# First steps of attention loaded in fp32 on the hardware queues, DMA issues pinned to program order, and w_out held back

## The chip, the cores and the metric

The kernel runs on one core of one Trainium2 chip. The metric is the time of one execution on the device in microseconds (us); a median is over all timed runs of a kernel. Every job also ran the kernel before on the same chip. The profile is one execution; its span runs from the first instruction to the last and is about 1.7 us shorter than the time of the same execution. The profile's names for the engines are PE (matmuls), DVE (VectorE), ACT (ScalarE), POOL (GpSimd) and SP (SyncE, which here only issues DMAs). In its lines `ps_s` are the scores, `ps_o` the attention sums, `ps_h` the projection into 2048; `qT` and `xblk` are q and x after their transposes, `v_f` is v in fp32.

A run counts as slow when it is over 1.5% above the fastest of the same kernel. With one core there is no other die to compare with, so this goes by the times alone.

## The reference, cut to what matters

```python
# q, k, v: (4, 8, 768, 64); window 128, 4 sink positions
scores = q @ k.T / sqrt(64)
keep   = (pos < 4) | ((0 <= rel) & (rel < 128))
x      = softmax(where(keep, scores, -1e9)) @ v      # -> (3072, 512)
h      = x @ w_in                                    # 512 -> 2048
P      = a0 + a1*h + a2*h**2 + a3*h**3
Q      = 1 + |b0|*|h| + |b1|*h**2
out    = (P / (Q + 1e-6)) @ w_out                    # 2048 -> 512
```

The output is 3072 x 512 in fp32. The kernel computes in bf16.

## The kernel before

It works in 12 steps of 256 tokens, each cut into two "units". One loop iteration holds the scores of one step, the attention sums of an earlier one and the projections of earlier ones, so that all engines have work. A tile scheduler orders the instructions of each engine, and that order need not be the program's.

```python
def load_q(tile_i):                    # 24 tiles of 128 tokens; 3 buffers
    t_ = a_kv.tile([P, H, D], BF16, tag="q_bf", name="q_bf", bufs=3)
    nc.gpsimd.dma_start(out=t_, in_=q[b, :, T*P:(T+1)*P, :]...)   # fp32 -> bf16 in flight
# load_k: two DMAs per step, 2 buffers; load_v: eight DMAs per step, 3 buffers

def turn_q(tile_i):                    # a tile's buffer comes free when this has run
    nc.sync.dma_start_transpose(out=qT_fix[b % 2][:, :, T*P:(T+1)*P], in_=q_bf.pop(tile_i)...)

def turn_x(s, grp):                    # x of a step in two groups, two DMAs each
    for n in range(NTS):
        nc.sync.dma_start_transpose(out=xblk[s][:, 2*grp:2*grp+2, n*P:(n+1)*P],
                                    in_=x_n[s][:, n, grp*2*P:(grp+1)*2*P])

for i in range(-3, NU + 4):            # (cut; s_q, s_a: steps of scores and of attention)
    if grp_q == 0: feed(s_q + 2)       # loads of k and two q tiles
    scores(s_q, 2 * grp_q)
    project_in(i, 0); attend(s_a, 2 * grp_a)
    scores(s_q, 2 * grp_q + 1)
    project_in(i, 1); attend(s_a, 2 * grp_a + 1)
    turn_x(s_a, grp_a)
    if grp_q == 0: load_v(s_q + 1)
    mask(s_q, grp_q)
    ...
    if grp_q == 1:                     # the last thing before the next step's scores
        turn_q(2 * s_q + 3); turn_q(2 * s_q + 4)
        turn_k(s_q + 1)
    ...
```

The softmax here doesn't subtract the row's maximum and nothing guards it: scores larger than these inputs give would overflow.

Of the kernel before, what the change touches and what calls it, by code (L numbers as in the profile page):

```python
# [9 lines left out]
FP32 = mybir.dt.float32  # L10
BF16 = mybir.dt.bfloat16
U32 = mybir.dt.uint32
AF = mybir.ActivationFunctionType
# [4 lines left out]
def kernel(  # L18
# [13 lines left out]
    nc = tc.nc  # L32
    nc.scalar.preload_act_table_set("natural_log_exp_and_others")

    B, H, S, D = q.shape
    NS = int(n_sink)
    P = 128
    DM = moe_w_in.shape[0]
    DF = moe_w_in.shape[1]
    NDMC = DM // P  # L40
    NFFC = DF // P
    NPB = H // 2
    TS = 256
    GPB = S // TS
    NSTEP = B * GPB
    NTS = TS // P
    NHF = TS // 64
    EW = 256
    UC = NFFC // 2
    UW = UC * TS  # L50
    NU = 2 * NSTEP
    inv_sqrt_d = 1.0 / float(D) ** 0.5

    const_pool = ctx.enter_context(tc.tile_pool(name="const", bufs=1))
    wpool = ctx.enter_context(tc.tile_pool(name="weights", bufs=1))
    a_kv = ctx.enter_context(tc.tile_pool(name="a_kv", bufs=2))
# [8 lines left out]
    ps_mp = ctx.enter_context(tc.tile_pool(name="ps_m", bufs=2, space=bass.MemoryType.PSUM))  # L65


    k_bf, v_bd, q_bf, qT_b = {}, {}, {}, {}
    v_fix = []
    for n in range(3):  # L70
        t_ = const_pool.tile([P, NPB, NHF, 2, D + 1], BF16, name=f"v_bd_{n}")
        nc.gpsimd.memset(t_, 0.0)
        for e in range(2):
            nc.gpsimd.memset(t_[e * 64:(e + 1) * 64, :, :, e, D:D + 1], 1.0)
        v_fix.append(t_)

    def load_q(tile_i):
        b, T = divmod(tile_i, S // P)
        t_ = a_kv.tile([P, H, D], BF16, tag="q_bf", name="q_bf", bufs=3)
        nc.gpsimd.dma_start(out=t_, in_=q[b, :, T * P:(T + 1) * P, :].rearrange("h p d -> p h d"))  # L80
        q_bf[tile_i] = t_

    def load_k(s):
        b, g = divmod(s, GPB)
        t_ = a_kv.tile([P, NTS, H * D], BF16, tag="k_bf", name="k_bf")
        for t in range(NTS):
            r0 = g * TS + t * P
            nc.gpsimd.dma_start(out=t_[:, t, :].rearrange("p (h d) -> p h d", h=H),  # L88
                                in_=k[b, :, r0:r0 + P, :].rearrange("h p d -> p h d"))
        k_bf[s] = t_  # L90

    def load_v(s):
        b, g = divmod(s, GPB)
        t_ = v_fix[s % 3]
        for h in range(H):
            i, e = divmod(h, 2)
            nc.gpsimd.dma_start(  # L97
                out=t_[e * 64:(e + 1) * 64, i, :, e, 0:D],
                in_=v[b, h, g * TS:(g + 1) * TS, :].rearrange("(j p) d -> p j d", p=64))
        v_bd[s] = t_  # L100


    b_bc = const_pool.tile([P, 2], FP32, name="b_bc")
    nc.sync.dma_start(out=b_bc, in_=moe_b.partition_broadcast(P))
    a_bc = const_pool.tile([P, 4], FP32, name="a_bc")
    nc.sync.dma_start(out=a_bc, in_=moe_a.partition_broadcast(P))

    for n in range(3):
        load_q(n)
    load_k(0)  # L110
    load_v(0)

    ident = const_pool.tile([P, P], BF16, name="ident")
    make_identity(nc, ident)

    edge = const_pool.tile([P, 2, 64], BF16, name="edge")
    nc.gpsimd.memset(edge, 1.0)
    for e in range(2):
        lo = e * 64
        nc.gpsimd.affine_select(  # L120
            out=edge[lo:lo + 64, 0, :], in_=edge[lo:lo + 64, 0, :], pattern=[[1, 64]],
            compare_op=ALU.is_ge, fill=0.0, base=0, channel_multiplier=-1)
        nc.gpsimd.affine_select(
            out=edge[lo:lo + 64, 1, :], in_=edge[lo:lo + 64, 1, :], pattern=[[-1, 64]],
# [49 lines left out]
    for grp in range(2):  # L174
        for n in range(2):
            t_ = const_pool.tile([P, 2 * NHF * EW + 64], BF16, name=f"e_{grp}_{n}")
# [3 lines left out]
    for n in range(2):  # L180
        t_ = const_pool.tile([P, NPB * NHF, P], BF16, name=f"kT_{n}")
# [3 lines left out]
    for n in range(2):  # L185
        t_ = const_pool.tile([P, NPB, P], BF16, name=f"k_sink_{n}")
        nc.vector.memset(t_, 0.0)
        k_sink.append(t_)
    qT_fix = []
    for n in range(2):  # L190
        t_ = const_pool.tile([P, NPB, S + P], BF16, name=f"qT_{n}")
# [8 lines left out]
    def load_w_in(half):  # L200
        f0, f1 = half * DF // 2, (half + 1) * DF // 2
        for c in range(NDMC):
            t_f = a_kv.tile([P, DF // 2], FP32, tag="w_in_f", name="w_in_f", bufs=2)
            nc.sync.dma_start(out=t_f, in_=moe_w_in[c * P:(c + 1) * P, f0:f1])
            nc.vector.tensor_scalar(out=w_in_sb[c][:, f0:f1], in0=t_f, scalar1=csc,
                                    scalar2=None, op0=ALU.mult)

    def load_w_out():
        for c in range(NFFC):
            nc.gpsimd.dma_start(out=w_out_sb[c], in_=moe_w_out[c * P:(c + 1) * P, :])  # L210

    def load_v_sink():
        for h in range(H):
            nc.gpsimd.dma_start(out=v_sink[16 * h:16 * h + NS, :, h, 0:D],
                                in_=v[:, h, 0:NS, :].rearrange("b s d -> s b d"))
        for b in range(B):
            nc.vector.tensor_copy(out=v_sink[:, b, :, D], in_=ind)


    def turn_q(tile_i):  # L220
        b, T = divmod(tile_i, S // P)
        nc.sync.dma_start_transpose(out=qT_fix[b % 2][:, :, T * P:(T + 1) * P],
                                    in_=q_bf.pop(tile_i).rearrange("p h d -> p (h d)"))

    def turn_k(s):
# [60 lines left out]
    x_n = {}  # L286
# [31 lines left out]
    xblk = {}  # L318

    def turn_x(s, grp):  # L320
        if grp == 0:
            xblk[s] = xpool.tile([P, NDMC, TS], BF16, tag="xblk", name="xblk")
        for n in range(NTS):
            nc.sync.dma_start_transpose(  # L324
                out=xblk[s][:, 2 * grp:2 * grp + 2, n * P:(n + 1) * P],
                in_=x_n[s][:, n, grp * 2 * P:(grp + 1) * 2 * P])

# [64 lines left out]
    def project_out(m, tt, part):  # L392
        if part == 0:
            ps_out[m, tt] = ps_mp.tile([P, DM], FP32, tag="ps_m", name="ps_out")
        for fc in range(part * UC, (part + 1) * UC):
            u, fl = divmod(fc, UC)
            co = fl * TS + tt * P
            nc.tensor.matmul(ps_out[m, tt], lhsT=g_of[m, u][:, co:co + P], rhs=w_out_sb[fc],  # L398
                             start=(fc == 0), stop=(fc == NFFC - 1))
        if part == 1:  # L400
            o_t = o_sb.tile([P, DM], FP32, tag="o_t", name="o_t")
            nc.scalar.activation(out=o_t, in_=ps_out[m, tt], func=AF.Copy)
            row0 = m * TS + tt * P
            nc.sync.dma_start(out=out[row0:row0 + P, :], in_=o_t)



# [3 lines left out]
    def feed(s):  # L411

        load_k(s)
        for n in (2 * s + 1, 2 * s + 2):
            if n < NQT:
                load_q(n)
# [2 lines left out]
    feed(1)  # L419
    load_v_sink()  # L420
    load_w_in(1)
    load_w_out()
    for n in range(3):
        turn_q(n)
    turn_k(0)
    for i in range(-3, NU + 4):
# [4 lines left out]
        has_m = 0 <= i < NU  # L431
        back = i - 3
        has_o = 0 <= back < NU
        if has_q and grp_q == 0 and s_q + 2 < NSTEP:
            feed(s_q + 2)
        if has_q:
            scores(s_q, 2 * grp_q)
# [25 lines left out]
        if has_m:  # L463
            magnitude(i)
            square(i)
            denominator(i)
        if has_o:
            project_out(back // 2, back % 2, 0)
        if has_q and grp_q == 0:
            sink_scores(s_q)  # L470
        if has_q and grp_q == 1 and s_q + 1 < NSTEP:
# [43 lines left out]
```

## Time and profile before

The kernel before took 321.15 us (median of 3 runs, 319.75 to 322.84). I cut its span by the starts of the Ln activations. Each of the 24 units has one: it is the first step of dividing P by Q. This gives five stages: the opening up to the first Ln, units 0 to 3, 3 to 12, 12 to 20, and the end.

The prediction shows the lines for them and says what limits them.

### The profile page before, as it was taken

How to read it: one execution, taken by the hardware profiler on the slowest of the kernel's cores; microseconds unless marked ns; L12 is line 12 of the kernel's file. 1: busy time of each engine (PE TensorE's matmuls, PEld its weight loads, DVE VectorE, ACT ScalarE, POOL GpSimd, SP SyncE). 2: the span in 40 equal slices, each digit the busy share in tenths (PEclk: the TensorE clock that was granted, in tenths of full speed). 3: DMA queues.
4: the chain of work that ended last, by engine and by line, in shares of the span. 5: the costliest groups of instructions: out<-in, count | busy, mean ns of one | idle time of the engine just before them, and what ended most of it. 6: DMA issues, size and time to landing. Idle time of an engine off the chain costs nothing.

```text
span 318.6 us, 5033 instructions
## 1 busy us (share of the span) xinstructions
PE 240.5 (75%) x1920; PEld 167.4 (53%) x1920; DVE 250.4 (79%) x384; ACT 212.8 (67%) x194; POOL 127.1 (40%) x192
## 2 busy tenths in 40 slices
PE   0025448749348969998879989989899898979964
PEld 0014336638224746666647665577575675746521
DVE  7534520769936897899998999999999899897990
ACT  1013014657823993996878978889799897877951
POOL 9986667996884341534540113356200000000000
PEclk9999556979858998999999999999999999999999
DMA  4999999999999996996960627549510111110011
GB/s 132 111 209 192 204 184 151 99 131 103 111 107 136 102 123 84 86 82 86 107 76 17 76 54 56 72 58 107 72 44 22 36 51 49 35 33 33 35 66 66
DMA packets 110775, 28.67 MB, mean 90 GB/s; under 512 B 104608, under 2 KB 106656, under 8 KB 110752
## 3 DMA queue, kind: packets, MB, share of 16 engines
q0 software_dynamic: 78976, 11.56, 58.1%
q1 hardware_dynamic: 31776, 16.79, 23.6%
q8 instruction: 15, 0.25, 0.3%
q14 instruction: 8, 0.07, 0.1%
HBM read 27.30 MB, written 6.29 MB: 105 GB/s over the span
## 4 chain that ended last, share of the span: by engine, by line
DVE 33%; ACT 21%; DMA 19%; PE 10%; issue 7%; POOL 5%; SPq 3%; DVEq 0%; ACTq 0%; POOLq 0%
DMA xblk<-x_n 12%; ACT lnq L379 7%; ACT den L383 6%; DVE den L358 5%; DVE g L388 5%; PE ps_h L339 5%; DVE num L373 4%; DVE sq L370 4%; PE ps_out L398 3%; ACT e L274 3%; SPq L324 3%; DVE den L354 3%; ACT hb L342 3%; DVE num L362 2%; DMA q_bf<-in_q_dram 2%
## 5 line engine op out<-in xcount | busy, mean ns | idle before, releaser
L339 PE MATMUL ps_h<-xblk,w_in_sb 128*128 128x256 bf16 x768 | 98.0, 278 | 30.7 <-DMA xblk<-x_n 30.6
L339 PEld LDWEIGHTS <-w_in_sb 128*128 128x128 bf16 x768 | 74.4, 100 | 45.6 <-DMA xblk<-x_n 28.1
L398 PE MATMUL ps_out<-w_out_sb,g 128*128 128x512 bf16 x384 | 93.5, 391 | 3.7 <-DVE g L388 3.4
L97 POOL DMA_DIRECT2D v_bd<-in_v_dram x96 | 61.8, 663 | 55.4 <-PE ps_o L305 47.3
L274 ACT ACTIVATE e<-ps_s 128x768 bf16<-128x768 f32 x48 | 38.7, 806 | 53.2 <-PE ps_s L270 53.2
L342 ACT ACTIVATE hb<-ps_h 128x1024 bf16<-128x1024 f32 x48 | 48.7, 1018 | 21.1 <-PE ps_h L339 21.1
L398 PEld LDWEIGHTS <-g 128*128 128x128 bf16 x384 | 37.3, 101 | 44.0 <-issue 5.1
L379 ACT ACTIVATE lnq<-den,one_eps,qsc 128x2048 f32<-128x2048 bf16 x24 | 50.2, 2092 | 5.5 <-DVE den L358 5.5
L383 ACT ACTIVATE den<-lnq 128x2048 bf16<-128x2048 f32 x24 | 45.8, 1908 | 0.0
L270 PE MATMUL ps_s<-qT,kT 128*128 128x192 bf16 x192 | 27.4, 272 | 9.4 <-DVE kT L237 7.3
L305 PE MATMUL ps_o<-v_bd,e 128*128 128x130 bf16 x352 | 31.4, 226 | 3.0 <-DMA v_bd<-in_v_dram 1.8
L388 DVE TENSOR_TENSOR g<-num,den 128x2048 bf16<-128x2048 bf16 x24 | 29.4, 1223 | 5.4 <-ACT den L383 5.3
L358 DVE TENSOR_TENSOR den<-den,sq 128x2048 bf16<-128x2048 bf16 x24 | 29.4, 1223 | 2.5 <-ACT sq L348 2.0
L281 DVE TENSOR_TENSOR e<-e,edge 128x1024 bf16<-128x1024 bf16 x24 | 16.2, 675 | 17.7 <-ACT e L274 17.7
L373 DVE TENSOR_TENSOR num<-num,sq 128x2048 bf16<-128x2048 bf16 x24 | 29.3, 1222 | 0.4
L370 DVE TENSOR_TENSOR sq<-sq,hb 128x2048 bf16<-128x2048 bf16 x24 | 29.1, 1214 | 0.1
L305 PEld LDWEIGHTS <-e 128*128 128x128 bf16 x352 | 26.1, 101 | 5.2 <-issue 3.5
L88 POOL DMA_DIRECT2D k_bf<-in_k_dram x24 | 22.2, 931 | 15.9 <-PE ps_kT L232 14.9
L80 POOL DMA_DIRECT2D q_bf<-in_q_dram x24 | 21.7, 906 | 17.2 <-DMA qT<-q_bf 17.2
L270 PEld LDWEIGHTS <-kT 128*128 128x128 bf16 x192 | 18.0, 108 | 16.4 <-DVE kT L237 9.8
L348 ACT ACTIVATE sq<-hb 128x2048 bf16<-128x2048 bf16 x12 | 22.9, 1911 | 0.3
L232 PE MATMUL ps_kT<-ident,k_bf 128*128 128x128 bf16 x96 | 8.1, 233 | 19.9 <-POOL ident masks.py:199 18.9
(56 smaller groups left out, 224.1 us busy)
## 6 DMA issues: line engine op xcount, KB each, us to landing
out_dram<-o_t SPq DMA_DIRECT2D x24, 256.0 KB, 2.1
w_in_f<-in_moe_w_in_dram SPq DMA_DIRECT2D x8, 512.0 KB, 5.8
q_bf<-in_q_dram POOLq DMA_DIRECT2D x24, 128.0 KB, 4.8
k_bf<-in_k_dram POOLq DMA_DIRECT2D x24, 128.0 KB, 4.8
v_bd<-in_v_dram POOLq DMA_DIRECT2D x96, 32.0 KB, 3.8
w_out_sb<-in_moe_w_out_dram POOLq DMA_DIRECT2D x16, 128.0 KB, 6.7
xblk<-x_n SPq DMA_TRANSPOSE x48, 2.5
qT<-q_bf SPq DMA_TRANSPOSE x24, 4.0
```

The costliest lines, as they stand in the source:

```text
L97: nc.gpsimd.dma_start(out=t_[e * 64:(e + 1) * 64, i, :, e, 0:D], in_=v[b, h, g * TS:(g + 1) * TS, :].rearrange("(j p) d -> p j d", p=64))
L270: nc.tensor.matmul(ps[:, n // 2, (n % 2) * 192:(n % 2) * 192 + 192], lhsT=kT_fix[s % 2][:, i * NHF + n, :], rhs=qT_fix[b % 2][:, i, c:c + ...
L274: nc.scalar.activation(out=data.rearrange("p (a n) c -> p a n c", a=2), in_=ps[:, :, 0:384].rearrange("p a (n c) -> p a n c", n=2), func=A ...
L305: nc.tensor.matmul(ps_o[:, n, :], lhsT=l_, rhs=r_.rearrange("p e c -> p (e c)"), start=(m == 0), stop=(m == len(terms) - 1))
L339: nc.tensor.matmul(ps_h[:, n, :], lhsT=w_in_sb[c][:, fc * P:(fc + 1) * P], rhs=xblk[m][:, c, :], start=(c == 0), stop=(c == NDMC - 1))
L342: nc.scalar.activation(out=hb[i][:, half * w:(half + 1) * w], in_=ps_h.rearrange("p n c -> p (n c)"), func=AF.Copy)
L358: nc.vector.tensor_tensor(out=den[i], in0=den[i], in1=sq[i], op=ALU.add)
L373: nc.vector.tensor_tensor(out=num[i], in0=num[i], in1=sq[i], op=ALU.add)
L379: nc.scalar.activation(out=lnq[i], in_=den[i], func=AF.Ln, scale=qsc, bias=one_eps)
L383: nc.scalar.activation(out=den[i], in_=lnq[i], func=AF.Exp, scale=-1.0)
L388: nc.vector.tensor_tensor(out=g_of[m, u], in0=num[i], in1=den[i], op=ALU.mult)
L398: nc.tensor.matmul(ps_out[m, tt], lhsT=g_of[m, u][:, co:co + P], rhs=w_out_sb[fc], start=(fc == 0), stop=(fc == NFFC - 1))
```

## The change

The intent is to take the first loads off POOL's queue: there the first q load went out at 6.82 us, and SP's first `w_in` at 1.73. k and v of steps 0 to 2 and q tiles 0 to 6 come in fp32 through SP and ACT and are cast on DVE and ACT. The first five q tiles and x of steps 0 and 1 are turned on PE. `w_out` waits until k of step 2 has been cast. And the DMA issues on SP and POOL are pinned to the order of the program, so that the scheduler cannot shuffle them. The issues of v on ACT's queue are not pinned. Smaller parts, partly outside the cut below: the fp32 buffers of `w_in` go from 2 to 4, the identity for the PE transposes is made before v's buffers are zeroed, k of step 2 and its q tiles are loaded ahead of the loop, and the first halves of the last projection are emitted earlier.

```diff
+    def pin(issue):
+        return lambda **kw: tc.keep_in_program_order(issue(**kw))
...
+    NS_HW = 3
+    NQ_HW = 7
+    NS_PE = 2
+    NQ_PE = 5
...
     def load_q(tile_i):
-        nc.gpsimd.dma_start(out=t_, in_=q[b, :, T * P:(T + 1) * P, :].rearrange("h p d -> p h d"))
+        src = q[b, :, T * P:(T + 1) * P, :].rearrange("h p d -> p h d")
+        if tile_i < NQ_HW:
+            f_ = a_kv.tile([P, H, D], FP32, tag="q_f", name="q_f", bufs=3)
+            pin(nc.sync.dma_start)(out=f_, in_=src)
+            nc.scalar.activation(out=t_, in_=f_, func=AF.Copy)
+        else:
+            pin(nc.gpsimd.dma_start)(out=t_, in_=src)
...
     def load_k(s):              # the same, with SP and a cast on DVE (k_f, bufs=1) for s < NS_HW
...
     def load_v(s):
+        if s < NS_HW:
+            f_ = a_kv.tile([P, NPB, NHF, D], FP32, tag="v_f", name="v_f", bufs=1)
...
+            if s < NS_HW:
+                nc.scalar.dma_start(out=f_[lo:hi, i], in_=src)
+            else:
+                pin(nc.gpsimd.dma_start)(out=t_[lo:hi, i, :, e, 0:D], in_=src)
...                              # and two casts on DVE
     def load_w_out():
+        gate = const_pool.tile([P, 1], BF16, name="gate")
+        pin(nc.gpsimd.tensor_copy)(out=gate, in_=gate_tile[NS_HW - 1][:, 0, 0:1])   # k2, cast
         for c in range(NFFC):
-            nc.gpsimd.dma_start(out=w_out_sb[c], in_=moe_w_out[c * P:(c + 1) * P, :])
+            pin(nc.gpsimd.dma_start)(out=w_out_sb[c], in_=moe_w_out[c * P:(c + 1) * P, :])
...
     def turn_q(tile_i):
-        nc.sync.dma_start_transpose(out=qT_fix[b % 2][:, :, T * P:(T + 1) * P],
+        if tile_i < NQ_PE:       # 4 transposes on PE, one copy on DVE
+            ...
+            return
+        pin(nc.sync.dma_start_transpose)(out=qT_fix[b % 2][:, :, T * P:(T + 1) * P],
...
     def turn_x(s, grp):
+        if s < NS_PE:            # 4 transposes on PE, one copy on DVE
+            ...
+            return
         for n in range(NTS):
-            nc.sync.dma_start_transpose(
+            pin(nc.sync.dma_start_transpose)(
...
     load_w_in(1)
+    feed(2)
     load_w_out()
...
-        if has_o:
+        if has_o and back < NU - 2:
             project_out(back // 2, back % 2, 0)
+        if i == NU:
+            for tt in range(NTS):
+                project_out(NSTEP - 1, tt, 0)
```

More of the change, by code (lines that the diff above doesn't have):

```diff
@@ L71 @@
         t_ = const_pool.tile([P, NPB, NHF, 2, D + 1], BF16, name=f"v_bd_{n}")
-        nc.gpsimd.memset(t_, 0.0)
-        for e in range(2):
-            nc.gpsimd.memset(t_[e * 64:(e + 1) * 64, :, :, e, D:D + 1], 1.0)
         v_fix.append(t_)
@@ L85, in load_k @@
         t_ = a_kv.tile([P, NTS, H * D], BF16, tag="k_bf", name="k_bf")
+        if s < NS_HW:
+            f_ = a_kv.tile([P, NTS, H * D], FP32, tag="k_f", name="k_f", bufs=1)
         for t in range(NTS):
             r0 = g * TS + t * P
-            nc.gpsimd.dma_start(out=t_[:, t, :].rearrange("p (h d) -> p h d", h=H),
-                                in_=k[b, :, r0:r0 + P, :].rearrange("h p d -> p h d"))
+            src = k[b, :, r0:r0 + P, :].rearrange("h p d -> p h d")
+            if s < NS_HW:
+                pin(nc.sync.dma_start)(out=f_[:, t, :].rearrange("p (h d) -> p h d", h=H), in_=src)
+            else:
+                pin(nc.gpsimd.dma_start)(out=t_[:, t, :].rearrange("p (h d) -> p h d", h=H),
+                                    in_=src)
+        if s < NS_HW:
+            nc.vector.tensor_copy(out=t_, in_=f_)
+            gate_tile[s] = t_
         k_bf[s] = t_
+    gate_tile = {}
     def load_v(s):
@@ L94, in load_v @@
         t_ = v_fix[s % 3]
+        if s < NS_HW:
+            f_ = a_kv.tile([P, NPB, NHF, D], FP32, tag="v_f", name="v_f", bufs=1)
         for h in range(H):
             i, e = divmod(h, 2)
-            nc.gpsimd.dma_start(
-                out=t_[e * 64:(e + 1) * 64, i, :, e, 0:D],
-                in_=v[b, h, g * TS:(g + 1) * TS, :].rearrange("(j p) d -> p j d", p=64))
+            lo, hi = e * 64, (e + 1) * 64
+            src = v[b, h, g * TS:(g + 1) * TS, :].rearrange("(j p) d -> p j d", p=64)
+            if s < NS_HW:
+                nc.scalar.dma_start(out=f_[lo:hi, i], in_=src)
+            else:
+                pin(nc.gpsimd.dma_start)(out=t_[lo:hi, i, :, e, 0:D], in_=src)
+        if s < NS_HW:
+            for e in range(2):
+                lo, hi = e * 64, (e + 1) * 64
+                nc.vector.tensor_copy(out=t_[lo:hi, :, :, e, 0:D], in_=f_[lo:hi])
         v_bd[s] = t_
     b_bc = const_pool.tile([P, 2], FP32, name="b_bc")
-    nc.sync.dma_start(out=b_bc, in_=moe_b.partition_broadcast(P))
+    pin(nc.sync.dma_start)(out=b_bc, in_=moe_b.partition_broadcast(P))
     a_bc = const_pool.tile([P, 4], FP32, name="a_bc")
-    nc.sync.dma_start(out=a_bc, in_=moe_a.partition_broadcast(P))
+    pin(nc.sync.dma_start)(out=a_bc, in_=moe_a.partition_broadcast(P))
+    ident = const_pool.tile([P, P], BF16, name="ident")
+    make_identity(nc, ident)
+    for n in range(3):
+        nc.gpsimd.memset(v_fix[n], 0.0)
+        for e in range(2):
+            nc.gpsimd.memset(v_fix[n][e * 64:(e + 1) * 64, :, :, e, D:D + 1], 1.0)
+    load_k(0)
     for n in range(3):
         load_q(n)
-    load_k(0)
     load_v(0)
-    ident = const_pool.tile([P, P], BF16, name="ident")
-    make_identity(nc, ident)
     edge = const_pool.tile([P, 2, 64], BF16, name="edge")
@@ L202, in load_w_in @@
         for c in range(NDMC):
-            t_f = a_kv.tile([P, DF // 2], FP32, tag="w_in_f", name="w_in_f", bufs=2)
-            nc.sync.dma_start(out=t_f, in_=moe_w_in[c * P:(c + 1) * P, f0:f1])
+            t_f = a_kv.tile([P, DF // 2], FP32, tag="w_in_f", name="w_in_f", bufs=4)
+            pin(nc.sync.dma_start)(out=t_f, in_=moe_w_in[c * P:(c + 1) * P, f0:f1])
             nc.vector.tensor_scalar(out=w_in_sb[c][:, f0:f1], in0=t_f, scalar1=csc,
@@ L208, in load_w_out @@
     def load_w_out():
+        gate = const_pool.tile([P, 1], BF16, name="gate")
+        pin(nc.gpsimd.tensor_copy)(out=gate, in_=gate_tile[NS_HW - 1][:, 0, 0:1])
         for c in range(NFFC):
-            nc.gpsimd.dma_start(out=w_out_sb[c], in_=moe_w_out[c * P:(c + 1) * P, :])
+            pin(nc.gpsimd.dma_start)(out=w_out_sb[c], in_=moe_w_out[c * P:(c + 1) * P, :])
     def load_v_sink():
         for h in range(H):
-            nc.gpsimd.dma_start(out=v_sink[16 * h:16 * h + NS, :, h, 0:D],
+            pin(nc.gpsimd.dma_start)(out=v_sink[16 * h:16 * h + NS, :, h, 0:D],
                                 in_=v[:, h, 0:NS, :].rearrange("b s d -> s b d"))
@@ L221, in turn_q @@
         b, T = divmod(tile_i, S // P)
-        nc.sync.dma_start_transpose(out=qT_fix[b % 2][:, :, T * P:(T + 1) * P],
+        if tile_i < NQ_PE:
+            qb = q_bf.pop(tile_i).rearrange("p h d -> p (h d)")
+            ps = ps_mp.tile([P, 512], FP32, tag="ps_m", name="ps_qT").bitcast(BF16)
+            ps = ps[:, 0:NPB * P].rearrange("p (i c) -> p i c", i=NPB)
+            for i in range(NPB):
+                nc.tensor.transpose(ps[:, i, :], qb[:, i * P:(i + 1) * P], ident)
+            nc.vector.tensor_copy(out=qT_fix[b % 2][:, :, T * P:(T + 1) * P], in_=ps)
+            return
+        pin(nc.sync.dma_start_transpose)(out=qT_fix[b % 2][:, :, T * P:(T + 1) * P],
                                     in_=q_bf.pop(tile_i).rearrange("p h d -> p (h d)"))
@@ L322, in turn_x @@
             xblk[s] = xpool.tile([P, NDMC, TS], BF16, tag="xblk", name="xblk")
+        if s < NS_PE:
+            ps = ps_mp.tile([P, 512], FP32, tag="ps_m", name="ps_xT").bitcast(BF16)
+            ps = ps[:, 0:2 * TS].rearrange("p (i c) -> p i c", i=2)
+            for il in range(2):
+                for n in range(NTS):
+                    c0 = (2 * grp + il) * P
+                    nc.tensor.transpose(ps[:, il, n * P:(n + 1) * P],
+                                        x_n[s][:, n, c0:c0 + P], ident)
+            nc.vector.tensor_copy(out=xblk[s][:, 2 * grp:2 * grp + 2, :], in_=ps)
+            return
         for n in range(NTS):
-            nc.sync.dma_start_transpose(
+            pin(nc.sync.dma_start_transpose)(
                 out=xblk[s][:, 2 * grp:2 * grp + 2, n * P:(n + 1) * P],
@@ L403, in project_out @@
             row0 = m * TS + tt * P
-            nc.sync.dma_start(out=out[row0:row0 + P, :], in_=o_t)
+            pin(nc.sync.dma_start)(out=out[row0:row0 + P, :], in_=o_t)
     NQT = B * (S // P)
@@ L433 @@
         has_o = 0 <= back < NU
-        if has_q and grp_q == 0 and s_q + 2 < NSTEP:
+        if has_q and grp_q == 0 and 3 <= s_q + 2 < NSTEP:
             feed(s_q + 2)
```

## The prediction

> **What bounds the kernel now.** I read the page's slices first, to see whether one limit holds throughout. Each digit is a slice of 8 us.
>
> ```profile
> span 318.6 us, 5033 instructions
> ...
> PE   0025448749348969998879989989899898979964
> ...
> DVE  7534520769936897899998999999999899897990
> ...
> PEclk9999556979858998999999999999999999999999
> DMA  4999999999999996996960627549510111110011
> ```
>
> There are two regimes. From slice 15 on DVE is at 9 nearly always and the DMA engines empty. Before that the DMA row is full, no compute engine is, and the PE clock falls to 5 tenths for long stretches. To cut the run into stages I took the starts of the Ln activations, one for each of the 24 half-steps ("units": two per step of 256 tokens): 61.12, 75.40, 84.39, 104.91 for units 0 to 3, 198.92 for unit 12, 278.34 for unit 20. The window view between these times (columns: length, then busy time of PE, PEld, DVE, ACT, POOL, clock, DMA share, GB/s):
>
> ```profile
> 0.00:61.12 61.12, 23.73 (x171) 18.09 (x172) 27.67 (x68) 13.52 (x16) 47.34 (x81) 0.83 1.30 162
> 61.12:104.91 43.79, 27.83 (x234) 20.41 (x233) 31.70 (x51) 25.24 (x25) 32.85 (x46) 0.81 1.71 120
> 104.91:198.92 94.01, 84.08 (x699) 58.59 (x698) 86.34 (x126) 78.53 (x73) 32.27 (x44) 0.98 0.78 78
> 198.92:278.34 79.42, 74.15 (x640) 52.93 (x638) 75.42 (x112) 69.29 (x64) 14.68 (x22) 1.00 0.36 54
> 278.34:318.60 40.26, 30.68 (x189) 17.41 (x186) 29.28 (x32) 26.22 (x21) 0.00 (x0) 1.00 0.14 49
> ```
>
> DVE is 95% busy from 198.92 to 278.34: 8 units in 79.42 us, 9.93 each, the floor of this design. From unit 3 to 12 a unit takes 94.01/9 = 10.45 us (DVE 92%). Units 0 to 3 take 14.6 each (DVE 72%), and the first Ln comes only at 61 (DVE 45%). So the excess over the floor is in the first 105 us: 43.79 - 3 x 9.93 = 14.0 us between units 0 and 3, and whatever of the 61 us of opening can go. What the engines wait for there is in the list of waits (total us, times, longest):
>
> ```profile
> ACT e L274 <- PE ps_s L270: 53.2, 17, 19.4
> ...
> PE ps_h L339 <- DMA xblk<-x_n: 30.6, 14, 8.9
> ...
> PE ps_kT L232 <- POOL ident masks.py:199: 18.9, 1, 18.9
> ...
> POOL q_bf L80 <- DMA qT<-q_bf: 17.2, 7, 5.2
> ```
>
> The chain of waits says which of these carry the end:
>
> ```profile
> 23.60 7.18 DMA q_bf<-in_q_dram
> 31.06 2.57 DMA v_sink<-in_v_dram
> ...
> 37.17 7.10 DMA xblk<-x_n
> ...
> 50.66 6.87 DMA v_bd<-in_v_dram
> ...
> 62.21 5.51 DMA xblk<-x_n
> ...
> 86.41 5.75 DMA xblk<-x_n
> ...
> 98.10 4.10 DMA xblk<-x_n
> ```
>
> The transpose of x by DMA takes 7.10, 5.51, 5.75 and 4.10 us while loads are in flight, and 2.3 to 2.4 after 143 us. [...] behind a late x the scores stand too: hence the 53.2 us that the exponentials wait.
>
> [...] a q tile costs POOL 0.896 us to issue and a v piece 0.637, and the landing of x stretches while POOL's loads run. [...] the kernel before does this for w_in already (8 tiles, 765 ns each, on DVE). [...] Here the clock was 0.50 from 34 to about 53 us[...]. [...] the k transposes here show it, 8 on PE and 1.39 us of copies.
>
> **The change part by part.**
>
> *Loads.* k and v of steps 0 to 2 and q tiles 0 to 6 leave POOL for SP (k, q) and ACT (v). POOL loses 6 x 0.9 + 7 x 0.9 + 24 x 0.64 = 27 us of issue, all early. The first load goes out at about 1.7 us, where SP issues w_in now, not at 6.8, behind POOL's memsets (5.5 us). The number of rows moved is the same (64 contiguous elements each). Estimate of the rate: between 9 and 10 us, with three q loads alone in flight, 105 GB/s were written in packets of 125 B (0.82 MB in 6563 packets over the first 20 us), some 840 packets/us; w_in alone ran at 340 to 350 GB/s. I assume 800 packets/us for the fp32 form too, an assumption that no trace here shows. Then k0, v0, q0 to 2 (7168 packets, 9 us) and four w_in tiles (2 MB, 6 us) are in by about 19 us; k1, v1, q3, q4 (6144, 7.7 us) by 27; the other w_in by 33; k2, v2, q5, q6 by 41, of which k2 lands at 36 to 38.
>
> *Casts.* DVE gets 3 casts of k (0.75 each, by the w_in row), 6 of v halves (0.7), 5 copies of turned q and 4 of x (0.4, by x_n): 2.3 + 4.2 + 2.0 + 1.6 = 10 us. ACT gets 7 casts of q (0.6, as the o_t row of the same size) and 24 issues (0.45, as SP's): 15 us. Nearly all lie before unit 1, where both idle more than half the time.
>
> *Order.* The list of DVE's instructions of the built kernel is what decides[...]. It has the cast of k0, of v0, the small setup (7 us), four w_in, cast of k1, q copies, then two of the second four w_in BEFORE the copies of kT of step 0, and the cast of k2 BEFORE the first x_n. So the first scores, at 22.1 us now, wait for a w_in landing near 29, and come at about 32; mask at 36; the k2 cast at 38; x_n of step 0 (34.5 now) at about 39. That is later than before. From there it gains: two x transposes on PE and a copy, under 1.5 us, in place of 35.22 to 49.58 for the four DMA transposes. Both groups of x0 are turned at about 46. Then 16 matmuls (2 to 4 us by the clock), two evictions, Square 1.91, den 1.23: first Ln at 57, against 61.12. Gain 4.
>
> *x of step 1 on PE, 8 x and 5 q transposes taken off the SP queue.* This removes the 5.51 us wait and, for step 2, the four q transposes that stood ahead of x on SP (8.49 us from 76.5). Units 0 to 3 should become DVE-bound: 31.7 us busy now, plus 0.8 (x copies) and 1.4 (v2 casts) is 34, at 97% busy 35. Gain 9.
>
> *Pinned order and w_out held back.* w_out is needed first at 93.7 us now; its gate opens with the k2 cast at 38, the 16 loads take 14 us as now (32 to 46). POOL then brings k3 and later in order, about 15 us ahead of need. q no longer runs ahead, so fewer loads meet the x transposes of units 3 to 12: 94 becomes 92. But what q does not load early comes later, and units 12 to 20 get it: 79.4 becomes 80. Gain 1.5.
>
> *Tail.* The first halves of the last projection are emitted earlier, but in both orders exactly 16 matmuls (3.63 us) follow the last gate. Gain 0 to 0.5.
>
> Sum: 57 + 35 + 92 + 80 + 40 = 304 us of span. The profiled run had 320.28 for a span of 318.6, so 305.5 is the time, about 5% less.
>
> **The rivals.** *The in-order stall eats the opening.* If fp32 rows move at 550 packets/us or SP takes 1 us to issue each, k2 lands at 45, x0 comes at 53 and the first Ln at 65 or later: about 313. For it: the two casts that stand ahead of what the path needs. Against: nothing in the profile shows such a slow rate. *The DMA load only moves.* The same bytes are read; if w_out, k3 and v3 at 40 to 85 us now stretch x of step 2 to 5 us twice and starve POOL's loads, units 3 to 12 keep their 94 or get worse: 309 to 314. For it: DMA share 1.71 in that stage. Against: three of the loads of that stage have been brought forward. *All goes well.* The first Ln at 50 and 10 us per unit from there: 50 + 30 + 90 + 80 + 40 plus 1.7, about 292. For it: the floor of 9.93 is shown later in the same trace, and the counts of early tiles look tuned. Against: the DVE order.
>
> **Range and chances.** 305.5, with 296 to 313 eight times in ten: the first Ln carries plus or minus 5, the stage to unit 3 plus or minus 3, the rest plus or minus 3. 2% faster is 314.7, outside the upper rival: faster 0.91, same 0.07, slower 0.02.
>
> **What would show it.** Right: no wait of PE on x before unit 4; first Ln near 57 and the first mask late, behind a w_in or k2 landing; units 0 to 3 in about 35; the stretch to the end as before within 3 us. Wrong: a first Ln past 62 (rate or order), PE waiting on x or v_bd again between 80 and 120 (moved load), or POOL's later loads coming late for units 5 to 20. If units 12 to 20 change by more than 3 us, the floor was not DVE's.

Passages on how the hardware behaves that no trace or run of this case shows are cut above, marked. In the paragraph on the cost of an issue, "does this" means casting on the chip, and "show it" means that the output of transposes on PE is then copied by DVE. That the new loads could not be cast in flight was not shown; that the change casts them on DVE and ACT is in the diff. In the kernel before, at the clock of 0.50 from 34 to 53 us, PE was busy for 11.16 of the 19 us; it was busy throughout 50 to 54, and from 54 to 56 the clock was 1.00. That engines keep to their lists was an assumption. The 0.7 us for a cast of half a v is an estimate with no row named; measured was 0.69 (median of six).

## More of the kernel before

One more view matters for what follows, and the prediction used it only for step 2: the issues on SP's queue (start, duration, queue and source line, operation, output and input, count).

```profile
76.53 8.49 SPq L222 DMA_TRANSPOSE qT<-q_bf  x4
...
100.83 11.29 SPq L222 DMA_TRANSPOSE qT<-q_bf  x5
```

Here the scheduler puts q transposes four or five in a row, well ahead of their scores. That delays an x now and then, but no scores ever wait for a q.

## The result, and the profile after

The changed kernel took 355.81 us (median of 4 runs, 350.71 to 358.03; the kernel before on that chip 321.41). The ratio is 1.0975, with a 95% interval of 1.0836 to 1.1113. A ratio here is the mean time of one kernel's fast runs over that of the other's fast runs of the same rounds, so it is not quite the ratio of the medians. The prediction, 305.5 us and 296 to 313, was wrong in sign.

The profiled run of the changed kernel (358.03) is one of its two slow runs. This does not carry the argument. Its fast runs took 350.71 and 354.64, and two fast profiles below (pins added to the kernel before; more q buffers) show units 3 to 12 and 12 to 20 within 7 us of its own.

The window view by stage; columns as in the prediction: length, busy time of PE, PEld, DVE, ACT and POOL, clock, DMA share, GB/s.

```profile
0.00:67.63 67.63, 24.13 (x208) 19.50 (x209) 36.69 (x86) 17.47 (x23) 28.57 (x55) 0.92 1.01 179
67.63:100.93 33.30, 26.23 (x233) 20.05 (x232) 31.44 (x51) 25.26 (x25) 10.03 (x14) 0.90 0.63 54
100.93:215.20 114.27, 91.00 (x683) 64.89 (x690) 86.14 (x125) 78.80 (x73) 35.20 (x50) 0.91 0.65 71
215.20:314.60 99.40, 82.79 (x642) 59.83 (x649) 74.68 (x111) 70.31 (x65) 26.29 (x39) 0.90 0.52 60
314.60:356.30 41.70, 32.04 (x178) 17.75 (x180) 29.21 (x32) 25.81 (x21) 0.00 (x0) 0.96 0.13 48
```

The first Ln comes 6.5 us later, units 0 to 3 are 10.5 us shorter, and the end is about the same. The loss lies in the middle: 213.7 us in place of 173.4 for units 3 to 20. DVE has the same work there (161 to 162 us busy in both kernels), but it is no longer the limit. The slices of the page (about 9 us each) show the holes right to the end:

```profile
DVE  4673733799887769887686496495576897987791
...
PEclk9999995999698989998898898898878999998999
```

The list of waits for the whole run (total us, times, longest):

```profile
POOL q_bf L37 <- DMA qT<-q_bf: 119.6, 7, 20.4
DVE rec L359 <- PE ps_o L353: 52.5, 23, 5.7
...
PE ps_h L397 <- DMA xblk<-x_n: 23.5, 9, 4.4
PE ps_s L318 <- DMA qT<-q_bf: 16.3, 12, 2.8
```

DVE now waits for attention sums on PE, and PE waits for two kinds of transposes by DMA. The same list for units 3 to 20 alone says how much of the 40.2 us each is:

| units 3 to 20 | before | after | difference |
|---|---|---|---|
| PE waits for q turned (`qT`) | none | 13.1 | +13.1 |
| PE waits for x turned (`xblk`) | 9.4 | 21.1 | +11.7 |
| PE busy, same matmuls | 158.2 | 173.7 | +15.5 |
| sum | | | +40.3 |

PE's other waits came to 5.8 us before and 5.7 after. PE is busy for longer with the same work because its clock drops after many of these waits: in units 3 to 20 the clock record of the trace has 11 spells at 0.50, 41 us in all, and that of run 1 below, without pins, has none. One such wait ends at 256.4. The first line below is the window right after it, the second an undisturbed one; the seventh figure, after the five pairs of busy times, is the clock:

```profile
256.40:259.60 3.20, 3.13 (x16) 2.27 (x17) 0.00 (x0) 0.00 (x0) 3.20 (x6) 0.50 1.18 76
...
231.50:234.10 2.60, 2.60 (x33) 2.42 (x31) 2.46 (x4) 2.46 (x3) 0.00 (x0) 1.00 0.04 9
```

The clock halves here again and again: after a wait of 4.42 us it is 0.50, and 14 matmuls of `ps_h` take 3.17 us. Another group of 14, at 146.71, takes 1.70: the wait of 2.24 us before it left the clock at 1.00. But most drops here follow shorter waits than 4.42 us: before seven of the 11 none was longer than 2.7 us, and before the one at 111.73 there were two waits of 0.95 and 1.05 us and 0.5 us of a third. In this trace ten of these spells at 0.50 last 3.41 us and one 6.83, and the drops lie whole multiples of 3.41 us apart. I cut units 3 to 20 into stretches of that length which end at the drops: in the one before each drop PE was idle for 2.1 to 3.3 us in sum, in those after which the clock stayed at 1.00 for at most 1.5 us. The 2.24 us before 146.71 fell across two of them, 1.39 and 0.85.

Why do the transposes come late? These are SP's issues in one step of the steady stage:

```profile
235.47 2.46 SPq L37 DMA_TRANSPOSE xblk<-x_n  x2
238.03 2.52 SPq L37 DMA_TRANSPOSE qT<-q_bf  x2
...
249.01 2.48 SPq L37 DMA_TRANSPOSE xblk<-x_n  x2
```

This is program order: `turn_x` of group 0, then the `turn_q` pair, which the loop writes directly ahead of the next scores. So a q tile that has long been loaded is turned only when x of the step before exists: the last q load before this pair was issued at 222.37, and no q load on POOL's queue in this run took over 11.9 us to land, so it was there before this x was even issued. The scores that need it resume at 241.88, after the pair has landed. Only then is the q buffer free, and POOL, pinned too, has stood at the next q load with everything else behind it. Its issues:

```profile
241.00 1.04 POOL L37 DMA_DIRECT2D q_bf<-in_q_dram  x1 [17.54 <-DMA qT<-q_bf]
242.03 4.93 POOL L37 DMA_DIRECT2D v_bd<-in_v_dram  x8
246.86 1.86 POOL L37 DMA_DIRECT2D k_bf<-in_k_dram  x2
248.61 0.99 POOL L37 DMA_DIRECT2D q_bf<-in_q_dram  x1
249.48 4.54 POOL L37 DMA_DIRECT2D v_bd<-in_v_dram  x7
```

POOL idles for 17.54 us and then issues a whole step's loads in one burst, into which the next x transposes (249.01) fall. The chain of waits shows the price (start, duration, what):

```profile
45.14 11.57 DMA v_f<-in_v_dram
...
239.34 2.50 DMA qT<-q_bf
...
250.24 6.19 DMA xblk<-x_n
256.47 3.17 PE ps_h L397 x14
```

That x takes 6.19 us, where one outside a burst (279.30, same chain) takes 2.35. The first of these lines belongs to the opening. A 64 KB piece of v of step 2 needs 11.57 us, beside the 16 loads of `w_out` that POOL issues from 40.7 on. DVE's cast of it stands ahead of the mask that attention needs (last bracket: idle before, and for what):

```profile
56.83 0.69 DVE L132 CAST v_bd<-v_f 64x1024 bf16<-64x1024 f32 x1 [7.92 <-DMA v_f<-in_v_dram]
```

This v was also issued late, from 37.46 to 47.00 on ACT's queue, because its only fp32 buffer came free with the casts of v of step 1 (the second at 36.73).

The theory after reading: the pins cost about 40 us in units 3 to 20, by tying the q transposes to x; and the gate of `w_out`, opened one load too early, costs about 8 us of the opening. The rivals: the head of POOL's queue alone (its wait for a q buffer, 119.6 us, is by far the longest line); or the fp32 loads and casts themselves.

### The profile page after: what moved, and what is told of

It reads as the page before. It is cut to its first block, busy times and chain, and to the rows that moved or that the text cites. A ratio compares the mean times of both kernels' runs of the same rounds, so it can differ in the third digit from the quotient of the medians.

```text
span 356.3 us, 5089 instructions
## 1 busy us (share of the span) xinstructions
PE 256.2 (72%) x1934; PEld 182.0 (51%) x1956; DVE 258.1 (72%) x402; ACT 217.7 (61%) x201; POOL 100.1 (28%) x156
## 4 chain that ended last, share of the span: by engine, by line
PE 28%; DVE 26%; DMA 24%; SPq 9%; ACT 7%; issue 4%; POOL 1%; ACTq 0%; DVEq 0%
PE ps_h L397 14%; DMA xblk<-x_n 9%; SPq L37 9%; DMA qT<-q_bf 6%; PE ps_o L353 5%; DMA v_f<-in_v_dram 5%; PE ps_out L456 5%; DVE num L431 4%; DVE sq L428 3%; PE ps_s L318 3%; DVE den L416 3%; DVE g L446 2%; DMA v_sink<-in_v_dram 2%; DVE x_n L361 2%; DVE e L329 2%
## 5 line engine op out<-in xcount | busy, mean ns | idle before, releaser
L397 PE MATMUL ps_h<-xblk,w_in_sb 128*128 128x256 bf16 x768 | 112.0, 301 | 23.8 <-DMA xblk<-x_n 23.5
L397 PEld LDWEIGHTS <-w_in_sb 128*128 128x128 bf16 x768 | 81.2, 108 | 42.7 <-DMA xblk<-x_n 25.9
L456 PE MATMUL ps_out<-w_out_sb,g 128*128 128x512 bf16 x362 | 89.5, 383 | 4.5 <-DVE g L446 1.6
L318 PE MATMUL ps_s<-qT,kT 128*128 128x192 bf16 x192 | 30.3, 284 | 33.2 <-DMA qT<-q_bf 16.3
L37 POOL DMA_DIRECT2D q_bf<-in_q_dram x17 | 16.2, 954 | 120.1 <-DMA qT<-q_bf 119.6
L359 DVE RECIPROCAL rec<-ps_o 128x4 f32<-128x4 f32 x48 | 8.6, 179 | 52.7 <-PE ps_o L353 52.5
L37 POOL DMA_DIRECT2D v_bd<-in_v_dram x72 | 45.3, 666 | 2.3 <-DMA q_bf<-in_q_dram 1.2
L353 PE MATMUL ps_o<-v_bd,e 128*128 128x130 bf16 x352 | 36.6, 246 | 8.7 <-DVE e L329 7.2
L353 PEld LDWEIGHTS <-e 128*128 128x128 bf16 x352 | 30.1, 112 | 12.2 <-DVE e L329 8.1
L460 ACT ACTIVATE o_t<-ps_out 128x512 f32<-128x512 f32 x24 | 14.2, 591 | 13.9 <-PE ps_out L456 10.7
```

What stands on the lines that cost most here:

```text
L37: return lambda **kw: tc.keep_in_program_order(issue(**kw))
L318: nc.tensor.matmul(ps[:, n // 2, (n % 2) * 192:(n % 2) * 192 + 192], lhsT=kT_fix[s % 2][:, i * NHF + n, :], rhs=qT_fix[b % 2][:, i, c:c + ...
L353: nc.tensor.matmul(ps_o[:, n, :], lhsT=l_, rhs=r_.rearrange("p e c -> p (e c)"), start=(m == 0), stop=(m == len(terms) - 1))
L397: nc.tensor.matmul(ps_h[:, n, :], lhsT=w_in_sb[c][:, fc * P:(fc + 1) * P], rhs=xblk[m][:, c, :], start=(c == 0), stop=(c == NDMC - 1))
L456: nc.tensor.matmul(ps_out[m, tt], lhsT=g_of[m, u][:, co:co + P], rhs=w_out_sb[fc], start=(fc == 0), stop=(fc == NFFC - 1))
```

## The experiments

All twelve kernels gave correct results. The first eight are changes of the changed kernel unless said otherwise. Stages are from the profiled run; the ratio is to the kernel before on the same chip.

| kernel | first Ln | 0 to 3 | 3 to 12 | 12 to 20 | end | median us | ratio |
|---|---|---|---|---|---|---|---|
| before | 61.1 | 43.8 | 94.0 | 79.4 | 40.3 | 321.15 | 1 |
| changed | 67.6 | 33.3 | 114.3 | 99.4 | 41.8 | 355.81 | 1.0975 |
| 1 no pins | 67.2 | 41.1 | 91.5 | 80.3 | 40.5 | 322.21 | 1.0059 |
| 2 six q buffers | 63.1 | 36.7 | 118.9 | 97.6 | 42.0 | 363.31 | 1.1369 |
| 3 pins off on POOL | 64.7 | 35.7 | 111.3 | 94.3 | 40.5 | 347.41 | 1.0845 |
| 4 pins off on SP | 58.4 | 34.2 | 101.0 | 84.5 | 40.8 | 321.70 | 1.0027 |
| 5 before, pins added | 72.0 | 41.3 | 107.4 | 97.6 | 40.2 | 359.87 | 1.1209 |
| 6 pins in the opening only | 67.7 | 43.1 | 91.5 | 81.9 | 40.5 | 326.96 | 1.0196 |
| 7 q turned one unit earlier | 67.6 | 33.7 | 98.1 | 85.7 | 40.5 | 328.31 | (slow) |
| 8 x on PE throughout | 68.1 | 33.0 | 94.0 | 84.2 | 40.5 | 322.44 | 1.0062 |
| 9 = 8, v's fp32 buffer doubled | 61.0 | 33.0 | 93.5 | 84.4 | 40.4 | 311.96 | 0.9825 |
| 10 = 8, w_out gated on v2 | 57.8 | 33.5 | 93.5 | 84.2 | 42.1 | 311.94 | 0.9791 |
| 11 = 6, x of 5 steps on PE, buffer doubled | 60.3 | 31.7 | 91.4 | 79.4 | 39.3 | 304.13 | 0.9567 |
| 12 = 11 with the gate of 10 | 58.5 | 33.0 | 92.5 | 79.3 | 39.3 | 304.67 | 0.9529 |

### 1: no pins

```diff
-        return lambda **kw: tc.keep_in_program_order(issue(**kw))
+        return issue
```

> The changed kernel with all pins taken off (the scheduler orders the DMA issues again), everything else kept. Theory 1 (the pinned order costs the time, from unit 3 on): units 3 to 20 fall back from 213.7 us to about 175, PE's waits for transposed q (16.3 us) go to near 0 and the time comes to 305 to 318. Theory 2 (the casts and the held w_out of the opening cost it): first Ln stays near 67 and the time stays within 345 to 358.

Measured: 322.21 us (321.57 to 323.36), ratio 1.0059 (0.9985 to 1.0132). The time missed the 305 to 318 of theory 1, but the stage that it spoke of came as it said. Units 3 to 20 are back to 171.8 us from 213.7. So all of the middle's loss comes with the pins, and none with the fp32 loads and casts. The rest of the change, without pins, is worth nothing: units 0 to 3 gain 2.7 us on the kernel before, and the first Ln comes at 67.2, here with a late `w_in` in the chain (it lands at 40.6).

### 2: six q buffers, all pins kept

```diff
-        t_ = a_kv.tile([P, H, D], BF16, tag="q_bf", name="q_bf", bufs=3)
+        t_ = a_kv.tile([P, H, D], BF16, tag="q_bf", name="q_bf", bufs=6)
```

> The changed kernel, pins kept, q_bf with 6 buffers in place of 3, so that POOL's q loads need not wait for q transposes (119.6 us of POOL waits in the changed kernel). Head-of-line theory (v and k loads stand behind a q load that waits for the transpose, then burst into the x transposes): x waits of PE fall from 23.5 us to under 10, time 320 to 335. Queue-place theory (the pinned SP queue puts q transposes behind x, and that alone costs): PE still waits for qT, time stays above 340.

Measured: 363.31 us (360.03 to 366.39), ratio 1.1369. In the waits of units 3 to 20, POOL no longer waits for a q buffer at all and PE's waits for x fall to 6.9 us, but these are left:

```profile
POOL k_bf L37 <- PE ps_kT L280: 81.5, 6, 17.5
...
PE ps_s L318 <- DMA qT<-q_bf: 27.1, 11, 6.0
```

The longest wait of the list was removed and the kernel became slower. POOL now stands at the next k instead (81.5 us), but by then the q tiles are in, and x is hardly late any more. So the rival that POOL's queue alone is to blame falls. PE waits for the turned q instead of x, because SP issues the turn in the same place as before. The 27.1 us here and the 13.1 + 21.1 us of the changed kernel are different mixtures of the same late issue.

### 3 and 4: pins off on POOL alone, and on SP alone

```diff
-            pin(nc.gpsimd.dma_start)(...)        # run 3: all of POOL's pins
+            nc.gpsimd.dma_start(...)
-            pin(nc.sync.dma_start_transpose)(...)    # run 4: all of SP's pins
+            nc.sync.dma_start_transpose(...)
```

> The changed kernel with the pins taken off POOL only; SP stays pinned. If the place of the q transposes in SP's queue is the root: time stays above 340, PE still waits for qT. If POOL's order mattered as much: below 335.

> The changed kernel with the pins taken off SP only (transposes, outputs, HW loads); POOL stays pinned. If the place of the q transposes in SP's queue is the root (they also release POOL's q loads): PE's wait for qT is gone, POOL's wait falls below 60 us, time 305 to 325. If the root is POOL's own pinned order: time above 335.

Measured: 347.41 us (347.05 to 348.24), ratio 1.0845 (1.0781 to 1.0909), without POOL's pins, where PE still waits 17.2 us for q in units 3 to 20; and 321.70 (320.60 to 327.12), ratio 1.0027, without SP's, where it no longer does. SP's pins carry most of it: against the mean of the changed kernel's fast runs, 352.7 us, taking them away gives about 31 us. Taking POOL's away gives about 5, and that is not clear of the noise, since its interval overlaps the changed kernel's. The two do not simply add up. Run 4 equals run 1 in time, but by a better opening (58.4 against 67.2) and a worse middle: 185.5 us against 171.8, with PE still waiting 19.5 us for x. POOL, still pinned, waits 81.5 us for k buffers there (the expectation had its wait below 60) and loads in bursts. So in the middle POOL's pins cost some 14 us even where SP is free. Run 4 also gives a first hint on the opening: there v of step 2 was in by 50 us.

### 5: the kernel before with pins added, and nothing else

```diff
-        nc.gpsimd.dma_start(...)     nc.sync.dma_start(...)     nc.sync.dma_start_transpose(...)
+        pin(nc.gpsimd.dma_start)(...)  pin(nc.sync.dma_start)(...)  pin(nc.sync.dma_start_transpose)(...)
```

> The kernel before with nothing but the pins added. Theory 1 (pins): slower by 20 to 45 us, that is 340 to 366, with PE waiting for qT and x each step. Theory 2 (casts, held w_out, PE turning are at fault): within 2% of before, 315 to 328.

Measured: 359.87 us (357.92 to 366.72), ratio 1.1209. Units 3 to 20 took 205.0 us, against 173.4 without pins, and in that stretch the waits are those of the changed kernel:

```profile
POOL q_bf L36 <- DMA qT<-q_bf: 94.6, 6, 17.5
...
PE ps_s L273 <- DMA qT<-q_bf: 11.4, 9, 2.1
```

The pins are enough to make the loss of the middle in a kernel that has no other part of the change. They also cost this kernel 10.9 us before the first Ln (72.0 against 61.1), which was not looked into.

### 6: pins in the opening only

```diff
+    opening = [1]
-        return lambda **kw: tc.keep_in_program_order(issue(**kw))
+        return lambda **kw: tc.keep_in_program_order(issue(**kw)) if opening else issue(**kw)
...
+    opening.clear()
     for i in range(-3, NU + 4):
```

> The changed kernel with pins only on what is emitted ahead of the loop (opening loads, w_out behind its gate, first q turns); in the loop the scheduler orders the issues. Theory: the opening's gain of the SP-free kernel (first Ln at 58.4, unit 3 at 92.6) plus the unpinned rest of the kernel before (94 + 79 + 40 us): 302 to 312. Rival, the opening's gain is always eaten by the loads that come later: 316 to 325.

Measured: 326.96 us (325.69 to 327.33), a miss. The middle was right (91.5 + 81.9), the start not: units 0 to 3 took 43.1 us. Free again, the scheduler put ten q transposes in a row ahead of the first x by DMA. They hold SP from 63.5 to 93.0, and PE waits up to 14.5 us for that x. The first Ln stayed at 67.7: `w_out` is gated as in the changed kernel, and DVE's cast of v of step 2 waits 8.4 us here too (the last of the pieces it needs lands at 57.3). So the order hurts in both directions: q too late behind x when pinned, x too late behind q when free.

### 7: pinned, but the q transposes written one unit earlier

```diff
             for n in (2 * s_q + 3, 2 * s_q + 4):
-                if n < NQT:              # just ahead of the next scores
+                if n < min(NQT, NQ_PE):  # the PE ones stay here
                     turn_q(n)
...
+        if has_q and grp_q == 0 and s_q + 1 < NSTEP:
+            for n in (2 * s_q + 3, 2 * s_q + 4):
+                if NQ_PE <= n < NQT:
+                    turn_q(n)            # two x groups ahead of them
```

> The changed kernel with all its pins; only the q transposes by DMA are written one unit earlier in the program, ahead of two groups of x. Queue-place theory: PE's wait for qT goes below 3 us and the time comes to 318 to 330, as with SP unpinned. If pinning costs by itself, whatever the order: above 340.

Measured: 327.30, 333.17, 329.33 and 321.21 us; all but the last count as slow, so there is no ratio, and the profile is of a slow run. With all pins kept, PE no longer waits for q at all and units 3 to 20 took 183.8 us. What is left is PE's wait for x, 17.3 us there, and a clock of 0.96. By this single profile the late q was the larger part of the loss; the bursts beside x are what is left to explain the rest.

### 8: pinned, x of all steps turned on PE

```diff
-    NS_PE = 2
+    NS_PE = 12
```

> The changed kernel with all its pins, but x of all 12 steps turned on PE (10 steps x 2 copies x 0.42 = 8.4 us more on DVE). q transposes then stand behind no x in SP's queue and no x waits for a DMA. Queue-place theory: PE waits neither for qT nor x; DVE-bound at about 10.4 us a unit: 312 to 330. If POOL's pinned order carries it: above 335.

Measured: 322.44 us (321.43 to 323.42), ratio 1.0062. The q transposes now stand behind no x, no x is caught in a burst, and no wait of PE on a transpose by DMA is left. Columns as above:

```profile
101.10:195.10 94.00, 86.36 (x747) 61.27 (x745) 89.46 (x134) 78.48 (x72) 40.30 (x55) 1.00 0.75 76
195.10:279.30 84.20, 77.94 (x673) 55.25 (x672) 80.30 (x122) 70.59 (x65) 24.04 (x34) 1.00 0.48 56
```

The clock is 1.00 and DVE is back at 95%. POOL still waits 77.8 us for q buffers in that stretch, which now costs nothing. The price is one more DVE copy per unit: 169.8 us of DVE in these stages against 161.2 in run 1, and the stages are 6.4 us longer than run 1's. The middle is thereby explained by two kinds of DMA transposes: q's, late by their place in SP's order, and x's, caught in the bursts of POOL's.

### 9 and 10: the opening, two cures of one suspected collision

Both start from run 8, whose opening is that of the changed kernel (first Ln at 68.1).

```diff
 # run 9: v of step 2 may be issued before v of step 1 is cast
-            f_ = a_kv.tile([P, NPB, NHF, D], FP32, tag="v_f", name="v_f", bufs=1)
+            f_ = a_kv.tile([P, NPB, NHF, D], FP32, tag="v_f", name="v_f", bufs=2)

 # run 10: the gate opens on the cast of v of step 2, not of k of step 2
-        pin(nc.gpsimd.tensor_copy)(out=gate, in_=gate_tile[NS_HW - 1][:, 0, 0:1])
+        pin(nc.gpsimd.tensor_copy)(out=gate, in_=v_fix[NS_HW - 1][:, 0, 0, 0, 0:1])
 # and load_w_out(), feed(3) are written after load_v(2)
```

> The same kernel with the fp32 buffer of v doubled (w_out's gate left on k2): v2 is then issued at about 16 to 27 us, before w_out. Both the collision and the late-issue theory say that the wait of the v2 cast goes: first Ln at 57 to 60, about 312. Rival (the opening is full anyway, v2's bytes move in front of k1, q3 to q6 and w_in and push the first scores back): first mask 2 to 5 us later than at 39, first Ln at 61 to 64, about 317.

> The kernel with x of all steps turned on PE (322.4 us, first Ln at 68.1), with one thing changed: the gate that holds w_out back opens on the cast of v2, not of k2. DVE's and ACT's orders are the same, and v2 is issued at the same time (37 to 47 us). Collision theory (v2's load took 8 to 11.6 us because the 16 w_out loads run beside it): v2 lands in under 4 us, the 8 us wait of the v2 cast goes, first Ln at 58 to 60, the other stages as they were (33, 94, 84, 40.5), about 313 us. Rival (v2 is late because ACT issues it late, between exponentials): v2 lands before 57 by 1 us at most, first Ln at 66 to 68, about 322. Third: the gain comes but k3, now behind w_out, is late: units 0 to 3 grow from 33 to 38 or more, and it is 317 to 319.

Measured: run 9 311.96 us (310.97 to 314.15), ratio 0.9825 (0.9706 to 0.9943); run 10 311.94 us (309.75 to 312.93), ratio 0.9791 (0.9652 to 0.9931). Both are faster than before, but neither interval is clear of the 2% mark, and the record calls both unclear. On this chip one run of the kernel before took 315.03 us, so that four of its seven runs count as slow; this holds for run 11 too. Run 10 is the one that tells the theories apart. DVE's and ACT's orders are those of run 8, and v of step 2 is issued at the same times (37.5 to 47.1 us), but `w_out` comes later. The cast:

```profile
48.91 0.68 DVE L132 CAST v_bd<-v_f 64x1024 bf16<-64x1024 f32 x1
```

It came at 57.55 in run 8 and no longer waits. The median landing of these eight pieces fell from 8.2 to 2.7 us, and the first Ln from 68.1 to 57.8. POOL issued nothing but `w_out` between 40.7 and 54.8 in run 8, so it is the neighbour that made the difference. The collision is shown, and the late issue alone is not the cause. The feared price, k of step 3 behind `w_out`, did not come: units 0 to 3 took 33.5 us. Run 9 gains less in the opening (first Ln at 61.0). Its first mask comes at 40.73 in place of 39.09, and `w_out` is released at 43.4 in place of 40.5. The likely reason, not tested, is its rival's: the bytes of v now come in front of others.

### 11 and 12: the parts that help, together

```diff
 # run 11: run 6 with
-    NS_PE = 2
+    NS_PE = 5
-            f_ = a_kv.tile([P, NPB, NHF, D], FP32, tag="v_f", name="v_f", bufs=1)
+            f_ = a_kv.tile([P, NPB, NHF, D], FP32, tag="v_f", name="v_f", bufs=2)
 # run 12: run 11, but bufs=1, and the gate and order of run 10 (load_w_out and feed(3) pinned)
```

> The best mix as far as the runs show it: pins in the opening only (there units 3 to 20 took 91.5 + 81.9), the fp32 buffer of v doubled, x of steps 0 to 4 on PE so that the q transposes which the scheduler puts ahead stand before no x that is needed. Theory: first Ln 58, units 0 to 3 34, 3 to 12 92, 12 to 20 81, end 40.5: span 305.5, time 307 us, 4.5% faster than before. Rival: the first x by DMA (step 5) still waits behind q transposes, or v3 and v4, which POOL now brings between q tiles, come late: units 3 to 12 take 97 to 100, about 314.

> The best kernel so far (304.1 us: pins in the opening only, x of steps 0 to 4 on PE) with the other cure of the opening: v's fp32 buffer back to one, and w_out's gate opening on the cast of v2 (which gave a first Ln at 57.8, where the doubled buffer gave 61.0 and, in the best kernel, 60.3). k3, q7 and q8 stay pinned behind w_out. If the two cures differ only in the opening: first Ln 57.8, then 32 + 91.5 + 79.5 + 39.5: span 300, time 302. Rival: w_out, issued from 50 to 60 us and k3 after it, now crowd units 0 to 3 and the first x by DMA: units 0 to 12 give back the 2.5 us, and it is 304 to 307.

Measured: run 11 304.13 us (303.63 to 304.46), ratio 0.9567 (0.9474 to 0.9661), which the record calls unclear although the interval lies below 0.98; run 12 304.67 us (304.07 to 307.68, 5 rounds), ratio 0.9529 (0.9481 to 0.9576), faster. Run 11's stages from the first Ln to unit 20:

```profile
60.30:92.10 31.80, 23.24 (x210) 16.96 (x209) 31.23 (x51) 24.24 (x23) 18.08 (x24) 0.95 1.50 109
92.10:183.50 91.40, 84.94 (x733) 60.75 (x732) 87.81 (x131) 79.77 (x74) 43.97 (x60) 1.00 0.94 87
183.50:262.90 79.40, 74.60 (x639) 53.43 (x638) 76.10 (x112) 69.57 (x64) 14.12 (x22) 1.00 0.36 55
```

DVE is at 96 to 98% from the first Ln to unit 20. With x of five steps on PE, the long row of q transposes stands before no x that is needed soon. Run 12's better opening (58.5) was given back in units 0 to 12, as its rival said: 125.5 us against run 11's 123.1. The two medians differ by 0.5 us on different chips, which decides nothing between them. Both beat the kernel before by over 4% and the changed kernel's fast runs by some 48 us.

## Why the prediction was wrong

*The step that failed* is "Pinned order and w_out held back", with its "94 becomes 92", its "79.4 becomes 80" and "Gain 1.5". Measured were 114.3 and 99.4, a loss of 40 us. The step looked at POOL's queue alone and took order for a good in itself: k3 in time, and no q running ahead of need. It did not ask what each pinned issue on SP waits for. The free scheduler's "q runs ahead" was a buffer of time between a load and its use; pinned, the turn of q sits behind an x that depends on the step just before, and directly ahead of the scores that need it (runs 1, 4 and 5 show that the pins, SP's above all, make the loss; runs 2 and 7 that it is the place of q's turn). The prediction listed the order of DVE's instructions in the built kernel, and got the opening's sequence from it. The same list for SP would have shown x, q, x in every step. It had also misread its own slices: it called the DMA engines empty from slice 15 on, where the row shows 6 or 9 in slices 15 to 20 and 4 to 9 in most up to slice 28 (about 230 us). So loads that can gather into bursts lie in all of units 3 to 12 and beyond. Its sentence "fewer loads meet the x transposes of units 3 to 12" was the reverse of what happened: the loads were not fewer but gathered into bursts.

*The first Ln* was mis-sized: 57 predicted, 67.6 measured. The sequence held. The cast of k2 came at 39.69 (38 predicted), the second copy of x0 at 48.49 (46 predicted). The missing term was the collision that the change itself makes: `w_out` was treated as 14 us of loads that nothing needs, and not as a neighbour of v of step 2. The prediction had this v in by 41, in one stream with k and q. It left out that the one fp32 buffer holds the issue back until 37.5 to 47.0, which put it beside `w_out`; it landed at 58.2. The assumed rate of the loads was not at fault: k of step 2 landed at 35.9 (36 to 38 predicted) and the last q tile at 38.3 (41). With the collision removed (run 10) the first Ln came at 57.8. So the 4 us gain was there, under a loss of 10.

*Units 0 to 3* were right: 35 predicted, 33.3 measured, and DVE at 94%. Turning x on PE did what it was meant to. A little of it is luck: DVE was busy for 31.4 us and not 34, partly because the late casts of v of step 2 (56.8 to 58.9) fell before the first Ln.

*The tail* was right in that nothing is gained: 41.8 us against 40.3.

*The sum* was 57 + 35 + 92 + 80 + 40 = 304; it became 67.6 + 33.3 + 114.3 + 99.4 + 41.8 = 356.4. Of the 52.4 us, 41.7 are units 3 to 20 (22.3 + 19.4) and 10.6 the opening; the other two terms cancel. Two smaller slips change nothing: the parts add up to 305.7 us of time and not 305.5; and of the 53.2 us that the exponentials waited, put down to late x, 19.4 is the wait for the very first scores, before there was any x.

*The rivals.* "The in-order stall eats the opening" named the right size for the first Ln, "65 or later", but for another reason: no slow rate, but one stretched load. "The DMA load only moves" had the right place and mechanism for a part of it, x stretched by loads that moved, but allowed it 3.5 to 8.5 us (309 to 314 against 305.5). None had q itself turned late, and all three stayed below 315. The prediction's own test did fire: units 12 to 20 changed by 20 us, so their floor was no longer DVE's.

*What stays open.* How the 15.5 us of slower PE divide between the waits for q and those for x was not measured by a run. An estimate from the clock record of the changed kernel: six of the 11 spells at 0.50 begin in or after waits of scores, five after waits for x, 20.5 us each, so about half and half. The scheduler's part was not measured either: pins also change where it puts other engines' instructions. Runs 7 and 8 show that with all pins kept and the two transposes out of each other's way the loss goes, which leaves little room for it.

## What to carry to other kernels

Before pinning an issue order, write out one period of each pinned queue and ask of every entry which data it waits for and who stands behind it; an order that is natural to write can put work that is ready behind work that is not, just ahead of its use (PE waited 13.1 us for q in units 3 to 20 of the changed kernel, and not at all in run 7, where only the place in the queue was changed). An engine's longest wait is not the cause for being longest: removing POOL's 119.6 us made the kernel slower. And a load that is held back is not free when it is released: open its gate on the last small load that is still on the path, which was worth 10 us here.
